# Attention in bursts of three throughout, and the first group's products in whole feature blocks of seven

## The chip, the cores and the metric

The kernel runs on one core of a Trainium2 chip. The metric is the device time of one execution in microseconds (us), the median of several runs.

## What is computed

Attention with a sigmoid in place of the softmax, then a bilinear feed-forward layer, all in float32:

```
scores = q @ kT / sqrt(64) - log(448)          # batch 8, heads 12, seq 448, head_dim 64
attn   = sigmoid(scores) @ v
x      = attn as (8*448, 12*64)                # 3584 tokens, d_model 768
out    = (((x @ w1) * (x @ w2)) @ w3) @ w_out  # d_ff 1024
```

## The kernel before

**Precision.** A float32 operand is split into a high and a low part of a reduced type (fp32r), and a product is three matmuls: high by high, high by low, low by high. One split is a cast (on ScalarE or VectorE, line 79) and a subtraction on VectorE (line 80).

**Attention** goes by items. A quad is four heads of one batch element (two pairs of heads), and there are 24 quads of seven items: three chunks of 128 keys for each pair, (0,0), (0,1), (0,2) and (1,0), (1,1), (1,2), and one short item `None`, the last 64 keys of all four heads, which stands fourth. An item has its scores (six matmuls on half the rows of the array, line 196; for the short one eight on quarter tiles, line 207) into a tile of two PSUM banks, one sigmoid of 128x896 on ScalarE (line 177) into a tile `a`, and its attend matmuls with v (four, line 220; short eight, line 228). The pool of `a` has four buffers.

**Bursts.** `sizes` cuts the 168 items into bursts. Burst k emits, in this order: the loads and splits of later pairs (`prepare`: the high cast of a pair is emitted with items (0,1) and (1,0), and its scores come three items later), the scores and sigmoids of its own items, the attends of the burst before it (`previous`), and a copy of a finished pair by ScalarE (`combine`, line 334), behind which products may follow. The order of all engines is written out by hand (`manual_schedule`): each engine works through its instructions in the order in which they are emitted.

**PSUM.** Eight banks: two `sp` tiles of two banks for scores, two `av` banks for the attends, and two upper banks. The upper pair is a tile `third` for the third item of a burst of three, or the two banks `up0` and `up1` of the products; `share_upper` closes the one pool and opens the other.

**Products** (`up`, line 533). Three of four groups of two batch elements go, as fillers, behind bursts. A group is eight feature blocks of seven products (a scheme of Strassen's kind with seven products for eight) of nine matmuls: 504 matmuls (`GROUP`). Results leave `up0`/`up1` by ScalarE copies (lines 542 and 548) and VectorE additions and multiplications (lines 500 and 503). The first group is spread over the bursts of `WINDOW`; groups 1 and 2 go whole behind the bursts of `blocks`; the last group follows the last burst.

**Weights.** w1 and w2 come as raw 64-bit words and are decoded, combined and split by the generator `weights`. One `next` is a unit: a VectorE step of the decoding (six steps for a matrix block, with the `magnitude` of the next block on ScalarE, line 89, in the fifth), a VectorE subtraction, or a `divide`: a 128x384 cast on ScalarE and a subtraction on VectorE, whose result fills one of ten slots. From the second feature block on, one block is 23 units:

```
s0 d0 t3 s1 t1 d2 s2 t2 n4 s3 d5 s4+m d1 s5 d3 | s0 d4 s1 s2 d6 s3 s4+m s5
```

Here s0 to s5 are decoding steps, m is the magnitude, t1, t2, t3 and n4 are subtractions, and d0 to d6 are the divides of the block before. 13 units lead (a start and the first block without divides) and a tail of 11 ends the 185. `take(stream, n)` takes n units. `beside` takes some behind each product. `change` holds the splits of attention results for the next group. The products of a block must find its seven divided weights, or `next(weights)` is called on the spot.

Of the kernel before, what the change touches and what calls it, by code (L numbers as in the profile page):

```python
# [25 lines left out]
def sigmoid_attention_bilinear_ffn(  # L26
# [162 lines left out]
    def scores(high, low, c, third, qk):  # L189

        at = c * P
        sp = score_banks(third)
        terms = ((high, high), (high, low), (low, high)) if high else ((qk, qk),)
        for m, (k, q) in enumerate(terms):
            for j, rows in enumerate(HEADS):
                nc.tensor.matmul(  # L196
                    sp[:, j], k[rows, 1, at:at + P], q[rows, 0],
                    start=m == 0, stop=m == len(terms) - 1,
                )
        return sp  # L200

    def short_scores(two, third):

        sp = score_banks(third)
        for u, qk in enumerate(two):
            for j, rows in enumerate(HEADS):
                nc.tensor.matmul(  # L207
                    sp[HEADS[u], j], qk[rows, 1, FULL:], qk[rows, 0], start=True, stop=True
                )
        return sp  # L210

    def attention(sp):
        a = pa.tile([P, 2, S], F32, name="a", bufs=4)
        sigmoid(a, sp)
        return a
# [18 lines left out]
    KH = NK // 2  # L234
# [111 lines left out]
    def prepare_weights():  # L346

        raw = {}

        def load(j):  # L350
            if j < 2 * NF:
                fc, i = divmod(j, 2)
                raw[j] = load_words(
                    words((w1, w2)[i], slice(fc * P, (fc + 1) * P)), p1, nc.gpsimd, 3
                )

        extras = iter(())
        for j in range(3):
            load(j)
        yield  # L360
        nxt = magnitude(raw[0], p1, 3)
        for fc in range(NF):
            fs = []
            for i in range(2):
                f = nxt
                j = 2 * fc + i
                fs.append(f)
                pops = POPS[i] if fc else (0,) * 6
                for step, _ in enumerate(decode(raw[j], f)):
                    if step == 4 and j + 1 < 2 * NF:  # L370
                        nxt = magnitude(raw[j + 1], p1, 3)
                    if step == 5:
                        del raw[j]
                        load(j + 3)
                    yield
                    for _ in range(pops[step]):
                        yield from one(extras)
            extras = finish_weights(fc, fs)
        for _ in range(sum(sum(pops) for pops in POPS)):
            yield from one(extras)  # L380
# [69 lines left out]
    def prepare_rest():  # L450

        raw = {}

        def load(i):
            if i < len(jobs):
                raw[i] = load_words(jobs[i][0], p2[0], nc.sync, 4)

        for i in range(3):
            load(i)
        for _ in range(6):  # L460
            yield
        f = magnitude(raw[0], p2[0], 3)
        for i, (_, dst) in enumerate(jobs):
            load(i + 3)
            for step, _ in enumerate(decode(raw.pop(i), f)):
                if step == 4 and i + 1 < len(jobs):
                    following = magnitude(raw[i + 1], p2[0], 3)
                yield
            nc.gpsimd.dma_start(out=dst, in_=f)
            f = following  # L470
# [3 lines left out]
    def up(g):  # L474
# [32 lines left out]
        for done, n in enumerate(stream[g * NF * 7:(g + 1) * NF * 7]):  # L507
# [55 lines left out]
            if not ending or done > 4:  # L563
                beside(g, n)
            yield

    def take(stream, n):
        done = 0
        for _ in itertools.islice(stream, n):
            done += 1  # L570
        return done
# [20 lines left out]
    assert len(quad) == TILES  # L592
    items = [(t, x) for t in range(B * NQ) for x in quad]
    GROUP = NF * 7 * KH * 3
    sizes = [3] * 18 + [2] * 28 + [3] * 5 + [2] + [3] * 5 + [2] + [3] * 8
    WINDOW = (18, 46)
    blocks = {51: 1, 57: 2}
    NBURST = len(sizes)
    starts = [sum(sizes[:k]) for k in range(NBURST + 1)]
    bursts = [items[i:i + n] for i, n in zip(starts, sizes)] + [[]]  # L600
# [3 lines left out]
    def beside(g, n):  # L604

        if g == 0:
            take(change, 1)
            take(weights, 2)
        elif not take(change, 1):
            take(rest, 2)  # L610

# [7 lines left out]
    weights = prepare_weights()  # L619
    for n in (2, 3):  # L620
        qks[n] = load_pair(n)
    filler = rest = iter(())
    change = Units(0)
# [23 lines left out]
    def attend_item(t, x, a):  # L647
        vv, vs = vvs[t]
        if x is None:
            two = (2 * t, 2 * t + 1)  # L650
            ends = [ends_of(n) for n in two]
            attend_short([accs[n] for n in two], vs, a, ends)
            for n in two:
                finish_given(n)
            return
        u, c = x
        n = 2 * t + u
        ends = ends_of(n)
        attend(accs[n], vv, u, c, a, *ends)
        finish_given(n)  # L660
        if (u, c) == (1, NC - 2):
            del vvs[t]

    def short_at(burst, at):

        shorts = [item for item in burst if item[1] is None]
        rest_of = [item for item in burst if item[1] is not None]
        if len(burst) == 3 and burst[1][1] is None:
            return shorts + rest_of if at == 0 else rest_of + shorts
        return list(burst)  # L670

    def prepare(t, x, hi_cast):

        if x == (0, 1):
            splits[2 * t + 1] = split_pair(qks[2 * t + 1], hi_cast)
        elif x == (0, 2) and t + 1 < B * NQ:
            vvs[t + 1] = load_v(t + 1)
        elif x == (1, 0) and t + 1 < B * NQ:
            splits[2 * t + 2] = split_pair(qks[2 * t + 2], hi_cast)
        elif x == (1, 1) and t + 2 < B * NQ:  # L680
            for n in (2 * t + 4, 2 * t + 5):
                qks[n] = load_pair(n)

    for k in range(NBURST + 1):
        if k == WINDOW[1]:
            phase_1.close()
            px.append(phase_x.enter_context(tc.tile_pool(name="px", bufs=1, side="left")))
            p2.append(phase_2.enter_context(tc.tile_pool(name="p2", bufs=2, side="right")))
            rest = prepare_rest()
        in_window = WINDOW[0] <= k < WINDOW[1]  # L690
        hi_cast = nc.scalar.copy if in_window or k in blocks else nc.vector.tensor_copy
        burst = bursts[k]
        for t, x in burst:
            prepare(t, x, hi_cast)
        if k < WINDOW[0]:
            if k == 1:
                next(weights)
            elif k > 1:
                take(change, 3)
                take(weights, 3 if k < 9 else 2 if k < 13 else 1)  # L700
        elif not in_window and k not in blocks and k < NBURST:
            take(change, 4 if k < 51 else 3)
        now = []
        for i, (t, x) in enumerate(short_at(burst, -1)):
            if x is None:
                sp = short_scores((qks.pop(2 * t), qks.pop(2 * t + 1)), i == 2)
            else:
                u, c = x
                if (k, i) == (0, 0):
                    high = low = None  # L710
                else:
                    high, low = splits[2 * t + u]
                sp = scores(high, low, c, i == 2, qks.get(2 * t + u))
            now.append((t, x, attention(sp)))
        if k == NBURST:
            take(change, 4)
            filler = up(NG - 1)
            take(filler, 9)
        by_place = {item[:2]: item for item in now}
        for item in previous:  # L720
            attend_item(*item)
        previous = [by_place[item] for item in short_at(burst, 0)]
        if k == WINDOW[0]:
            filler = up(0)
        if in_window:
            take(weights, 3 if k > WINDOW[0] + 1 else 0)
            done = k + 1 - WINDOW[0]
            if done % 2 == 0:
                upto, since = (GROUP * i // (WINDOW[1] - WINDOW[0]) for i in (done, done - 2))
                take(filler, upto - since)  # L730
            if k + 1 == WINDOW[1]:
                take(filler, 10)
                change = Units(1)
                take(weights, 10 ** 6)
                for n in range(RING - 1):
                    load_weights(NF * 7 + n)
        elif k in blocks:
            filler = up(blocks[k])
            take(filler, GROUP + 10)
            change = Units(blocks[k] + 1)  # L740
# [280 lines left out]
```

## Time and profile before

| | |
|---|---|
| median of three runs | 966.53 us (966.41 to 967.92) |
| the profiled execution's own time | 964.66 us |
| its span, first to last instruction | 962.9 us |
| TensorE (PE) busy | 955.6 us, 99% of the span |
| VectorE (DVE) busy | 657.1 us, 68% |
| ScalarE (ACT) busy | 400.2 us, 42% |

The median is the metric. The sum of the prediction is made against the profiled execution, whose time lies 1.76 us above its span and 1.87 us under the median. Matmul durations overlap in the trace: what one costs is read from start to start.

### The profile page before, as it was taken

The numbers are of one execution on the slowest core, as the hardware profiler recorded it, in microseconds if no ns is written. First come the engines' busy times: TensorE is split into PE (matmuls) and PEld (weight loads), VectorE is DVE, ScalarE is ACT, GpSimd is POOL, SyncE is SP. The second block draws the span as 40 slices with busy tenths as digits, with TensorE's granted clock in tenths as the row PEclk, the third lists the DMA queues.
The fourth block names the chain that finished last, engine by engine and source line by source line (L and its number), as shares of the span: only waits on it lengthen the run. The fifth ranks groups of instructions, "written<-read, shape, count | busy, mean of one in ns | idle before, by whom it ended". The sixth has DMA issues, their size and how long they took to land.

```text
span 962.9 us, 14120 instructions
## 1 busy us (share of the span) xinstructions
PE 955.6 (99%) x5236; PEld 756.4 (79%) x5236; DVE 657.1 (68%) x1060; ACT 400.2 (42%) x583; POOL 104.8 (11%) x182
## 2 busy tenths in 40 slices
PE   9999999999999999999999999999999999999998
PEld 5444666676674999957999747999999999999997
DVE  5869778887639788899888628444465657474752
ACT  7887456556548121263221474112243523232230
POOL 1110123222200012110111100211000000000000
PEclk9999999999999999999999999999999999999999
DMA  8864577776645899975999734988431033343402
GB/s 268 254 214 132 190 258 240 244 259 233 234 130 171 293 380 379 381 274 173 366 375 355 240 93 131 355 295 285 165 141 62 29 127 123 115 144 111 157 30 86
DMA packets 93781, 204.37 MB, mean 212 GB/s; under 512 B 9872, under 2 KB 57104, under 8 KB 93712
## 3 DMA queue, kind: packets, MB, share of 16 engines
q1 hardware_dynamic: 78432, 142.40, 44.0%
q0 software_dynamic: 15136, 60.83, 17.6%
q8 instruction: 42, 0.69, 0.3%
q10 hardware_dynamic: 144, 0.23, 0.1%
q14 instruction: 27, 0.22, 0.1%
HBM read 148.37 MB, written 55.05 MB: 211 GB/s over the span
## 4 chain that ended last, share of the span: by engine, by line
PE 95%; DVE 2%; DMA 1%; ACT 1%; issue 1%; SPq 0%; DVEq 0%; ACTq 0%
PE up L533 42%; PE av L220 11%; PE sp L196 8%; PE av L985 7%; PE sp L985 7%; PE up L985 7%; PE av L853 3%; PE sp L853 3%; PE av L228 2%; PE third L196 1%; PE sp L207 1%; DMA vv<-vL 1%; PE third L207 1%; ACT a L177 0%; DVE low L80 0%
## 5 line engine op out<-in xcount | busy, mean ns | idle before, releaser
L533 PE MATMUL up<-hS,w 128*128 128x448 f32 x702 | 214.6, 366 | 0.0
L533 PE MATMUL up<-hA,w 128*128 128x448 f32 x510 | 159.5, 367 | 0.3 <-ACT a L177 0.3
L177 ACT ACTIVATE a<-sp,bias 128x896 f32<-128x896 f32 x132 | 129.9, 1010 | 49.8 <-PE sp L196 24.6
L533 PEld LDWEIGHTS up<-hS,w 128*128 128x128 f32 x702 | 131.8, 188 | 14.7 <-issue 3.5
L533 PE MATMUL up<-lS,w 128*128 128x448 f32 x351 | 128.2, 365 | 0.0
L220 PE MATMUL av<-a,vv 128*64 128x448 f32 x576 | 122.8, 551 | 0.1
L533 PEld LDWEIGHTS up<-hA,w 128*128 128x128 f32 x510 | 95.8, 188 | 13.3 <-issue 4.5
L533 PE MATMUL up<-lA,w 128*128 128x448 f32 x255 | 93.2, 365 | 0.0
L220 PEld LDWEIGHTS av<-a,vv 128*64 128x64 f32 x576 | 35.5, 136 | 67.8 <-issue 67.3
L500 DVE TENSOR_TENSOR u<-up,p 128x448 f32<-128x448 f32 x64 | 39.9, 623 | 55.4 <-PE up L533 52.2
L542 ACT COPY p<-up 128x448 f32<-128x448 f32 x31 | 16.6, 534 | 146.8 <-PE up L533 141.5
L533 PEld LDWEIGHTS up<-lS,w 128*128 128x128 f32 x351 | 65.9, 188 | 5.2
L985 PE MATMUL av<-gh,wo 128*128 128x448 f32 x224 | 68.6, 367 | 0.0
L985 PE MATMUL sp<-gh,wo 128*128 128x448 f32 x224 | 68.6, 367 | 0.0
L985 PE MATMUL up<-gh,wo 128*128 128x448 f32 x224 | 68.5, 367 | 0.0
L500 DVE TENSOR_TENSOR u<-up,u 128x448 f32<-128x448 f32 x64 | 39.8, 622 | 32.4 <-PE up L533 31.8
L79 ACT CAST gh<-gf 128x896 fp32r<-128x896 f32 x40 | 35.7, 944 | 56.2 <-PE sp L985 50.0
L80 DVE TENSOR_TENSOR gl<-gf,gh 128x896 fp32r<-128x896 f32 x40 | 41.9, 1087 | 22.7 <-ACT gh L79 22.7
L80 DVE TENSOR_TENSOR low<-qk,high 128x896 fp32r<-128x896 f32 x47 | 51.3, 1091 | 7.4 <-ACT high L79 6.3
L89 ACT ACTIVATE f<-raw 128x768 f32<-128x768 f32 (+2 forms) x48 | 34.5, 718 | 50.5 <-DMA w_dram<-f 17.0
L196 PEld LDWEIGHTS sp<-high 64*128 64x128 f32 x232 | 21.9, 185 | 42.8 <-ACT a L177 31.0
L548 ACT COPY c<-up 128x448 f32<-128x448 f32 x31 | 16.6, 534 | 85.7 <-PE up L533 60.0
(145 smaller groups left out, 1778.3 us busy)
## 6 DMA issues: line engine op xcount, KB each, us to landing
w<-w_dram SPq DMA_DIRECT2D x168, 384.0 KB, 5.9
gf<-g_dram SPq DMA_DIRECT2D x16, 896.0 KB, 5.7
w_dram<-w POOLq DMA_DIRECT2D x36, 384.0 KB, 4.7
raw<-w POOLq DMA_DIRECT2D x16, 768.0 KB, 6.2
qk<-qT SPq DMA_DIRECT2D x48, 224.0 KB, 4.8
qk<-kT SPq DMA_DIRECT2D x47, 224.0 KB, 4.9
out<-o_sb SPq DMA_DIRECT2D x47, 224.0 KB, 2.0
vv<-vL SPq DMA_DIRECT2D x24, 384.0 KB, 3.5
```

The lines of the kernel that those rows point to most:

```text
L79: hi_engine(out=dst_hi, in_=src)
L80: lo_engine.tensor_tensor(out=dst_lo, in0=src, in1=dst_hi, op=ALU.subtract)
L89: nc.scalar.activation(f, raw[..., 1].bitcast(F32), AF.Abs, scale=HW_SCALE)
L177: nc.scalar.activation(dst, src, AF.Sigmoid, bias=bias[:n], scale=scale)
L196: nc.tensor.matmul(sp[:, j], k[rows, 1, at:at + P], q[rows, 0], start=m == 0, stop=m == len(terms) - 1,)
L207: nc.tensor.matmul(sp[HEADS[u], j], qk[rows, 1, FULL:], qk[rows, 0], start=True, stop=True)
L220: nc.tensor.matmul(acc[cols, :S], vv[:, c, at:at + D], a[:, j], start=start, stop=stop,)
L228: nc.tensor.matmul(acc[cols, :S], vs[HEADS[u], cols], a[HEADS[u], j], start=ends[u][0], stop=ends[u][1],)
L500: nc.vector.tensor_tensor(out=out, in0=a, in1=b, op=ALU.add)
L533: nc.tensor.matmul(a, w[:, i, kc], x, start=bool(start) and kc == 0 and m == 0, stop=bool(stop) and kc == KH - 1 and m == 2, skip_group_ch ...
L853: nc.tensor.matmul(acc, a[:, jc], w[:, jc, ms], start=(jc == 0 and m == 0), stop=(jc == NF - 1 and m == 2),)
L985: nc.tensor.matmul(acc, w[:, fc, ms], g[:, fc], start=start and fc == 0 and m == 0, stop=fc == NH - 1 and m == 2, skip_group_check=True,)
```

## The change

All bursts have three items (56 of them in place of 66). The window is 19 bursts, 18 to 36, in place of 28 bursts of two, and the first group's products are emitted as whole feature blocks, 63 matmuls each, behind bursts 19, 22, 24, 27, 29, 32, 34 and 36, in place of 36 matmuls behind every second burst. Groups 1 and 2 go behind bursts 42 and 48, of three items too, in place of bursts of two. Within the window four units of `weights` are taken behind each burst from the third on in place of three, and behind a product two, or one behind the last two products of a block.

```diff
-    sizes = [3] * 18 + [2] * 28 + [3] * 5 + [2] + [3] * 5 + [2] + [3] * 8
-    WINDOW = (18, 46)
-    blocks = {51: 1, 57: 2}
+    sizes = [3] * 56
+    WINDOW = (18, 37)
+    FIRST_BLOCKS = [WINDOW[0] + i - 1 for i in itertools.accumulate((2, 3, 2, 3, 2, 3, 2, 2))]
+    blocks = {42: 1, 48: 2}
...
         if g == 0:
             take(change, 1)
-            take(weights, 2)
+            take(weights, 2 if n % 7 < 5 else 1)
...
         elif not in_window and k not in blocks and k < NBURST:
-            take(change, 4 if k < 51 else 3)
+            take(change, 4 if k < 42 else 3)
...
         if in_window:
-            take(weights, 3 if k > WINDOW[0] + 1 else 0)
-            done = k + 1 - WINDOW[0]
-            if done % 2 == 0:
-                upto, since = (GROUP * i // (WINDOW[1] - WINDOW[0]) for i in (done, done - 2))
-                take(filler, upto - since)
+            take(weights, 4 if k > WINDOW[0] + 1 else 0)
+            if k in FIRST_BLOCKS:
+                take(filler, 7 * KH * 3)
             if k + 1 == WINDOW[1]:
                 take(filler, 10)
```

## Rows read from the trace of the kernel before

**Rows 1.** The page: the span, the busy time of three engines (time, share of the span, instructions), and the granted TensorE clock in 40 slices of the span, in tenths.

```profile
span 962.9 us, 14120 instructions
...
PE 955.6 (99%) x5236; PEld 756.4 (79%) x5236; DVE 657.1 (68%) x1060; ACT 400.2 (42%) x583; POOL 104.8 (11%) x182
...
PEclk9999999999999999999999999999999999999999
```

**Rows 2.** All waits of PE: the line that waited, the line waited for, us in total, how often, the longest.

```profile
PE up L586 <- DVE wo L579: 1.5, 1, 1.5
PE sp L196 <- DVE low L80: 0.9, 2, 0.5
PE sp L196 <- ACT a L177: 0.5, 1, 0.5
PE up L533 <- ACT a L177: 0.3, 1, 0.3
PE up L533 <- DVE c L500: 0.3, 1, 0.3
```

**Rows 3.** The window of the first group by stretches, busy time (and instructions) of each engine: from the first burst of two to the last, then the five bursts of three behind it.

```profile
88.70:286.70 198.00, 197.18 (x1118) 132.96 (x1117) 147.66 (x238) 114.55 (x169) 44.04 (x74) 1.00 0.66 221
286.70:309.00 22.30, 22.30 (x159) 10.78 (x158) 21.09 (x36) 19.34 (x28) 1.02 (x2) 1.00 0.53 170
```

**Rows 4.** PE in order of time (start, us, line, operation, count): two bursts of two, 36 products from 124.30 to 131.81, and the next bursts. The row of 135.78 holds a wait for a sigmoid.

```profile
121.23 0.47 PE L196 MATMUL sp<-high 64*128 64x448 f32 x2
...
122.65 1.72 PE L220 MATMUL av<-a,vv 128*64 128x448 f32 x8
124.30 0.47 PE L533 MATMUL up<-hS,w 128*128 128x448 f32 x1
...
131.81 0.98 PE L207 MATMUL sp<-qk 64*64 64x448 f32 x8
132.73 0.47 PE L196 MATMUL sp<-high 64*128 64x448 f32 x2
...
133.53 1.72 PE L220 MATMUL av<-a,vv 128*64 128x448 f32 x8
135.78 0.47 PE L196 MATMUL sp<-high 64*128 64x448 f32 x2 [0.53 <-ACT a L177]
136.09 0.36 PE L196 MATMUL sp<-low,high 64*128 64x448 f32 x2
...
138.39 0.97 PE L220 MATMUL av<-a,vv 128*64 128x448 f32 x4
139.29 0.47 PE L533 MATMUL up<-hA,wo 128*128 128x448 f32 x1
```

**Rows 5.** The chain of work that ended last: group 1's products (start, us, count).

```profile
313.08 102.39 PE up L533 x504
```

**Rows 6.** PE in order of time: a burst of three attended without a short item; then the last burst of three, its attends, and the first product of the last group behind it.

```profile
292.87 2.48 PE L220 MATMUL av<-a,vv 128*64 128x448 f32 x12
295.28 0.47 PE L196 MATMUL sp<-high 64*128 64x448 f32 x2
...
576.56 0.47 PE L196 MATMUL sp<-high 64*128 64x448 f32 x2
...
578.58 1.72 PE L220 MATMUL av<-a,vv 128*64 128x448 f32 x8
580.24 0.98 PE L228 MATMUL av<-a,vs 64*64 64x448 f32 x8
581.56 0.47 PE L533 MATMUL up<-hA,w 128*128 128x448 f32 x1 [0.34 <-ACT a L177]
```

**Rows 7.** ACT in order of time beside the same last burst: its three sigmoids.

```profile
578.07 1.00 ACT L177 ACTIVATE a<-sp,bias 128x896 f32<-128x896 f32 x1
579.60 1.01 ACT L177 ACTIVATE a<-sp,bias 128x896 f32<-128x896 f32 x1 [0.53 <-PE av L220]
580.51 1.00 ACT L177 ACTIVATE a<-third,bias 128x896 f32<-128x896 f32 x1
```

**Rows 8.** ACT in order of time: the copy of a pair, a magnitude and a weight cast between two bursts of three; a magnitude that waits for VectorE's subtraction; another such, a high cast and the sigmoids behind it.

```profile
50.52 0.53 ACT L334 COPY A<-av 128x448 f32<-128x448 f32 x1
50.94 0.94 ACT L89 ACTIVATE f<-raw 128x768 f32<-128x768 f32 x1
51.76 0.52 ACT L79 CAST w<-t 128x384 fp32r<-128x384 f32 x1
52.16 1.02 ACT L177 ACTIVATE a<-sp,bias 128x896 f32<-128x896 f32 x1
...
111.73 0.92 ACT L89 ACTIVATE f<-raw 128x768 f32<-128x768 f32 x1 [0.63 <-DVE wo L80]
...
133.04 0.95 ACT L89 ACTIVATE f<-raw 128x768 f32<-128x768 f32 x1 [1.30 <-DVE wo L80]
133.86 0.96 ACT L79 CAST high<-qk 128x896 fp32r<-128x896 f32 x1
134.69 1.93 ACT L177 ACTIVATE a<-sp,bias 128x896 f32<-128x896 f32 x2
```

**Rows 9.** Behind group 1's block: VectorE's last read of the product banks, and PE's first scores into `third`.

```profile
416.23 0.62 DVE L500 TENSOR_TENSOR u<-up,u 128x448 f32<-128x448 f32 x1
...
415.41 0.47 PE L196 MATMUL sp<-high 64*128 64x448 f32 x2
...
416.90 0.98 PE L207 MATMUL third<-qk 64*64 64x448 f32 x8
```

## Prediction

> **What bounds the kernel now.** The page first: TensorE (PE) is busy 955.6 of 962.9 us, the other engines far less, and the granted clock stands in its top tenth in every slice [rows 1]. So time can be won only by giving PE less to do, and is lost wherever PE waits. Its waits come second: 3.5 us in all, of which 0.5 us for a sigmoid, 0.3 us for a sigmoid ahead of products, and 0.3 us for a VectorE result [rows 2]. In the window of the first group PE has 0.82 us of idle time in 198.0 us, with VectorE busy 75% and ScalarE 58%; the five bursts of three behind it have none [rows 3]. The third view is PE in order of time, from which I take what a group of matmuls of one shape costs to enter, since that is all that cutting the same work into fewer bursts can save.
>
> **What the change saves on PE.** All matmuls stay. Scores of two items take 1.42 us (121.23 to 122.65), of one item 0.80 us (132.73 to 133.53): 0.62 us an item and 0.18 us to enter [rows 4]. Attends take 0.90 us for one item, 1.65 us for two [rows 4] and 2.41 us for three [rows 6]: 0.76 us an item, 0.14 us to enter. 36 products take 7.51 us [rows 4]; at 102.39/504 = 0.203 us each [rows 5] they are 7.31 us, so 0.20 us to enter. Bursts go from 66 to 56 and product blocks from 16 to 10: 10 x (0.18 + 0.14) + 6 x 0.20 = 4.4 us. The short items' own groups stay 24 and 24. Two waits of the window go with its bursts of two: the scores at 135.78 come 0.60 us after 133.53 + 1.65 [rows 4], and 0.3 us for VectorE [rows 2]. Saved: 5.3 us.
>
> The Trainium skill, "TensorEngine Tiling (Array Packing)", Tiling Modes (Key Properties), says that a change of tiling mode drains the array, and "TensorE: Matmul & The Clock Gate", Single matmul latency, puts the fixed part of one matmul at 166 ns. By these an estimate for the 26 groups saved is 4.3 us, where the rows give 4.4.
>
> **What it adds: products behind a burst of three.** Before, the window's bursts of two never touch the upper two banks, and both whole-group blocks stand behind bursts of two. After, each of the ten blocks follows a burst whose third scores lie in the two banks that its first product writes. So that product waits for the sigmoid that reads `third`. The trace shows this once, at the end: the first product of the last group starts at 581.56, after a wait for the sigmoid that ran from 580.51 to 581.51 [rows 6, 7].
>
> Why that sigmoid is late there, with nothing else on ScalarE: six tiles `a` would be alive (three to be attended, three being made), and there are four. The second sigmoid starts only at 579.60, 1.02 us after the attends began at 578.58, released by them, and the third 0.91 us later [rows 7]. So the third starts 1.93 us after the attends' start, and the product 2.98 us after it. The attends themselves last 2.41 us without a short item [rows 6], and with one 1.66 + 0.92 = 2.58 us, taking the short one at its score's 0.92 us [rows 4]. Least wait per block: 0.57 us without, 0.40 us with a short item. Block bursts 27, 32, 34 and 48 attend a short item, the other six don't: 4 x 0.40 + 6 x 0.57 = 5.0 us. With bursts of two there were four tiles for four, and nothing to wait for.
>
> **What else stands ahead of that sigmoid.** In the window the high cast of a pair is on ScalarE, and weight casts and magnitudes are emitted behind each burst, so ahead of the next burst's sigmoids. Before, the 36 products (7.5 us) gave ScalarE time to catch up; after, bursts of 4.4 to 4.7 us follow each other twice or three times. Start to start a pair's copy takes 0.42 us, a magnitude 0.82, a weight cast 0.40, a high cast 0.83 [rows 8], a sigmoid 0.91 [rows 7].
>
> Count from the start of a burst: scores end at 2.02 us (578.58 - 576.56 [rows 6]), or 2.32 with a short item scored; the third sigmoid is due 1.93 later, so the first may start as late as 2.14 (2.44) without harm. A burst on time leaves ScalarE at 4.86 (5.16), behind that come the copy, the burst's weight work and the next high cast, and PE goes on at scores + attends.
>
> The weight work follows from counting units: 35 are taken before the window, each block takes 12, each burst from 20 on four. That puts, per burst, a magnitude and two casts (1.62 us) at 20, 25, 28 and 31; a magnitude and one (1.22) at 33; three casts (1.20) at 35; two (0.80) at 23 and 26; one (0.40) at 21 and 30; none at 18. Worked through:
> - block 19: 4.86 + 0.42 + 0.83 - 4.60 = 1.51, below 2.44: on time.
> - 22: burst 21's first sigmoid at 4.86 + 0.42 + 1.62 + 0.83 - 4.60 = 3.13, its end 2.72 later at 5.85; 22's at 5.85 + 0.42 + 0.40 + 0.83 - 4.43 = 3.07: 0.63 late.
> - 24: 2.31, on time.
> - 27: burst 26 at 3.13, then 5.85 + 0.42 + 0.80 + 0.83 - 4.73 = 3.17 against 2.14: 1.03 late.
> - 29: 4.86 + 0.42 + 1.62 + 0.83 - 4.43 = 3.30: 0.86 late.
> - 32, without a high cast: 5.16 + 0.42 + 1.62 - 4.73 = 2.47: 0.33 late.
> - 34: 5.16 + 0.42 + 1.22 + 0.83 - 4.73 = 2.90: 0.76 late.
> - 36: 2.88: 0.44 late.
> - 42 and 48 have no weight work and fall under block 19's sum.
>
> Together 4.05 us. The bound below is nothing (ScalarE not late), the bound above adds a magnitude's wait for VectorE's subtraction just ahead of it, 0.63 us in one row, 1.30 in another, none in a third [rows 8]; three of the chains (bursts 25, 28, 33) hold that pair, so up to 3 x 0.63 = 1.9 us more. I take half, 0.95.
>
> ScalarE's casts stand in the way only because it keeps its order. The Trainium skill says so ("PSUM — Partial Sum Buffer", Engine vs sequencer instructions: ScalarE's queue is strict FIFO). By that rule the late part counts; an engine that took the sigmoid first would leave 5.0 - 5.3 = -0.3 us.
>
> **What I cost at nothing.** VectorE inside a block: its mean instruction is 147.66/238 = 0.62 us [rows 3], so an addition and two units behind each product are 1.86 us against 9 x 0.203 = 1.83 us of products, and the last two products take one unit less. It stays level; if each block's last addition came 0.62 us later, the next third scores would wait, since behind group 1's block the addition ends at 416.85 and those scores start at 416.90 [rows 9]: up to 8 x 0.62 = 5.0 us. Units: each block finds its weights, since before blocks 0 to 7 some 35, 59, 79, 103, 123, 147, 167 and 187 can have been taken, and the divides fall due at 33 + 23 per block, the last few of which `beside` supplies three or more products ahead. Loads per burst are those of the bursts of three behind the window, in which PE never idles [rows 3]. `change` is taken as often between the same events. The stores and the five weight loads at the window's end stand behind the last block on POOL and SP as before, with five bursts until group 1 needs them.
>
> **The sum.** Waits 5.0 + 4.05 + 0.95 = 10.0 us, saved 5.3: +4.7 us. The profiled execution of 964.66 us becomes 969.4; the median, 1.87 above it, 966.53 + 4.7 = 971.2 us.
>
> **The rivals.**
> - *Only the tile wait is paid* (ScalarE catches up in time): -0.3 us, 966.2. For it: ScalarE is busy only 58% of the window [rows 3]. Against: a magnitude and a high cast ahead of the sigmoids already made PE wait at 135.78 [rows 4, 8], with more room than there will be. With half the lateness: +1.7 us. 22%, no measurable change.
> - *The change wins its entries* (the other side): the waits stay under 3.4 us, since the sigmoid behind the block's burst is not late. Place: the first product of each block; it decides at 0.34 us per block, under the smallest wait of rows 6 and 7. With no wait at all, -5.3 us: 961.2. For it: 2 of the 10 blocks stood behind bursts without any wait before, though of two. Against: the row of 581.56. The Trainium skill ("Perfetto Trace Analysis", Matmuls) wants independent groups in different banks, so that one's evacuation overlaps the next; here the third item and the products share theirs, and the rule speaks for the wait. 12%.
> - *VectorE becomes late too*: blocks pay another 0.6 us at the third scores behind them, +9.7 us, 976.2. For it: no margin in rows 9. Against: one unit less behind the last two products. 10%.
> - My forecast, +2.5 to +7 us: 56%.
>
> **How the numbers follow.** About 0.2%, 1.9 us, is what can be told from no change: 964.6 to 968.5 counts as the same. Slower: 56 + 10 = 66%. Same: 22%. Faster: 12%. The range reaches from the lower edge of the tile-wait case, 964.8, to 975.5, short of the VectorE case; some 12% are left below it and 8% above. My own case alone spans 969.0 to 973.5.
>
> **What would show it.** Right: PE waits of products (line 533) for the sigmoid (line 177), ten of them besides the one at the end, near 10 us in all, from 0.4 to 0.6 us at blocks 19, 24, 42 and 48 to 1.4 or more at 27 and 29, where ScalarE shows magnitude, casts and high cast just ahead of the sigmoids. Scores groups 56, PE's busy time down some 4 us. The prediction is wrong if the first product of a block follows the attends at once, if these waits sum to 5 us (ScalarE not late), or if new waits stand elsewhere: third scores behind VectorE, or products behind weights.

## The result: 0.74% slower

The changed kernel takes 973.0 us (median of six, 970.05 to 975.37) against 965.96 us for the kernel before in the same comparison: ratio 1.0074, 95% interval 1.0059 to 1.0089, which is 5.7 to 8.6 us. The forecast was slower, +4.7 us and 971.2 us. The direction and the place are right, the size falls short, and the part that is missing was not among the rivals. Two executions among those of the experiments ran at a mean granted clock of 0.61 and 0.66 and took over 1330 us; no ratio below contains them.

The profiled execution took 970.05 us, 5.4 more than that of the kernel before. The page of the changed kernel, its span and the busy time:

```profile
span 968.3 us, 14147 instructions
...
PE 950.0 (98%) x5236; PEld 758.4 (78%) x5236; DVE 656.4 (68%) x1058; ACT 400.7 (41%) x585; POOL 104.4 (11%) x182
```

PE is busy 5.6 us less than in [rows 1], and idle 18.3 us where it was 7.3. Where the idle time came from is in the view of all waits of PE, laid out as [rows 2]:

```profile
PE up L533 <- ACT a L177: 10.7, 11, 2.2
PE up L586 <- DVE wo L579: 1.5, 1, 1.5
PE sp L196 <- DVE low L80: 0.9, 2, 0.5
PE third L196 <- DVE low L80: 0.6, 1, 0.6
PE third L196 <- ACT a L177: 0.6, 1, 0.6
PE up L533 <- DVE u L500: 0.3, 1, 0.3
PE sp L196 <- ACT a L177: 0.2, 1, 0.2
```

Eleven waits of products for a sigmoid, 10.7 us: ten blocks, and the one of 0.34 us at the end that was there before. PE in order of time, the first product of each block, with the idle time ahead of it in brackets, and one other pair of waits (89.73 and 90.76), to which I come back:

```profile
89.73 0.47 PE L196 MATMUL third<-high 64*128 64x448 f32 x2 [0.56 <-ACT a L177]
90.76 0.47 PE L196 MATMUL third<-low,high 64*128 64x448 f32 x2 [0.57 <-DVE low L80]
99.30 0.47 PE L533 MATMUL up<-hA,w 128*128 128x448 f32 x1 [0.56 <-ACT a L177]
127.22 0.47 PE L533 MATMUL up<-hA,wo 128*128 128x448 f32 x1 [1.11 <-ACT a L177]
150.18 0.47 PE L533 MATMUL up<-hA,w 128*128 128x448 f32 x1 [0.56 <-ACT a L177]
...
179.42 0.47 PE L533 MATMUL up<-hA,w 128*128 128x448 f32 x1 [1.35 <-ACT a L177]
...
204.39 0.47 PE L533 MATMUL up<-hA,wo 128*128 128x448 f32 x1 [2.23 <-ACT a L177]
...
232.09 0.47 PE L533 MATMUL up<-hA,w 128*128 128x448 f32 x1 [0.71 <-ACT a L177]
...
256.38 0.47 PE L533 MATMUL up<-hA,w 128*128 128x448 f32 x1 [1.88 <-ACT a L177]
...
279.63 0.47 PE L533 MATMUL up<-hA,wo 128*128 128x448 f32 x1 [0.96 <-ACT a L177]
...
320.95 0.47 PE L533 MATMUL up<-hA,w 128*128 128x448 f32 x1 [0.56 <-ACT a L177]
...
451.77 0.47 PE L533 MATMUL up<-hA,w 128*128 128x448 f32 x1 [0.40 <-ACT a L177]
```

The forecast for these ten, block by block, was 0.57, 1.20, 0.57, 1.43, 1.43, 0.73, 1.16, 1.01, 0.57 and 0.40 us. Eight of ten agree within 0.1 us. The two that don't are blocks 29 and 34, by 0.80 and 0.72 us. ACT in order of time ahead of block 29 says why:

```profile
196.88 1.00 ACT L177 ACTIVATE a<-third,bias 128x896 f32<-128x896 f32 x1
197.76 0.53 ACT L334 COPY A<-av 128x448 f32<-128x448 f32 x1
198.18 0.53 ACT L79 CAST w<-f 128x384 fp32r<-128x384 f32 x1
199.45 0.95 ACT L89 ACTIVATE f<-raw 128x768 f32<-128x768 f32 x1 [0.74 <-DVE w L80]
200.31 0.49 ACT L79 CAST w<-t 128x384 fp32r<-128x384 f32 x1
200.71 0.93 ACT L79 CAST high<-qk 128x896 fp32r<-128x896 f32 x1
201.55 1.88 ACT L177 ACTIVATE a<-sp,bias 128x896 f32<-128x896 f32 x2
203.34 0.99 ACT L177 ACTIVATE a<-third,bias 128x896 f32<-128x896 f32 x1
```

One burst's third sigmoid, a pair's copy, the weight cast, a magnitude that waits 0.74 us for VectorE's subtraction, a second cast, the high cast, and only then the three sigmoids of the block's burst, the last of which ends at 204.33. The product starts at 204.39.

### The profile page after: what moved, and what is told of

The parts are those of the page before. It is cut to its first block, busy times and chain, and to the rows that moved or that the text cites. A ratio compares the mean times of both kernels' runs of the same rounds, so it can differ in the third digit from the quotient of the medians.

```text
span 968.3 us, 14147 instructions
## 1 busy us (share of the span) xinstructions
PE 950.0 (98%) x5236; PEld 758.4 (78%) x5236; DVE 656.4 (68%) x1058; ACT 400.7 (41%) x585; POOL 104.4 (11%) x182
## 4 chain that ended last, share of the span: by engine, by line
PE 89%; ACT 5%; DVE 3%; issue 2%; DMA 1%; DVEq 0%; ACTq 0%
PE up L533 42%; PE av L220 7%; PE av L984 7%; PE sp L984 7%; PE up L984 7%; PE sp L196 6%; ACT a L177 4%; PE av L852 3%; PE sp L852 3%; PE third L196 2%; PE av L228 2%; PE third L207 1%; DMA w_dram<-w 1%; ACT high L79 1%; DVE low L80 1%
## 5 line engine op out<-in xcount | busy, mean ns | idle before, releaser
L177 ACT ACTIVATE a<-sp,bias 128x896 f32<-128x896 f32 x112 | 111.8, 1012 | 78.0 <-PE sp L196 39.7
L220 PE MATMUL av<-a,vv 128*64 128x448 f32 x576 | 120.6, 549 | 0.0
L177 ACT ACTIVATE a<-third,bias 128x896 f32<-128x896 f32 x56 | 56.4, 1007 | 0.0
L533 PEld LDWEIGHTS up<-lA,w 128*128 128x128 f32 x255 | 47.9, 188 | 3.6
```

Source lines behind the costliest of these rows:

```text
L177: nc.scalar.activation(dst, src, AF.Sigmoid, bias=bias[:n], scale=scale)
L220: nc.tensor.matmul(acc[cols, :S], vv[:, c, at:at + D], a[:, j], start=start, stop=stop,)
L533: nc.tensor.matmul(a, w[:, i, kc], x, start=bool(start) and kc == 0 and m == 0, stop=bool(stop) and kc == KH - 1 and m == 2, skip_group_ch ...
```

## The experiments

My theory: products wait for the sigmoid that reads the shared banks, held back partly by the four tiles `a` and partly by ScalarE's other work ahead of it. The rivals: whole blocks cost time by themselves (VectorE, weights), or the entries saved are worth less than read from the rows.

**High casts on VectorE.**

```diff
-        hi_cast = nc.scalar.copy if in_window or k in blocks else nc.vector.tensor_copy
+        hi_cast = nc.scalar.copy if k in blocks else nc.vector.tensor_copy
```

> The changed kernel with the high casts of the window's pairs on VectorE in place of ScalarE, blocks 42 and 48 as they are. Theory (two parts: four tiles of sigmoid results hold the third sigmoid back by 0.4 to 0.57 us per block, ScalarE's other work the rest): the late part falls by 0.83 us per burst, the waits of products from 10.7 to between 5.5 and 7 us, each of them 0.4 to 1.0 us; 4 to 5 us faster than the changed kernel, if VectorE's added 0.62 us per pair makes no new wait. Rival (ScalarE's order has nothing to do with it, only the tiles count): no change against the changed kernel.

Ratio to the kernel before 1.0037 (1.0022 to 1.0053): some 3.6 us faster than the changed kernel, a little under what was expected. PE's waits, and two first products in order of time, blocks 27 and 29:

```profile
PE up L533 <- ACT a L177: 7.1, 11, 1.4
```

```profile
178.39 0.47 PE L533 MATMUL up<-hA,w 128*128 128x448 f32 x1 [0.40 <-ACT a L177]
...
202.56 0.47 PE L533 MATMUL up<-hA,wo 128*128 128x448 f32 x1 [1.40 <-ACT a L177]
```

Block 27 falls from 1.35 us to its least wait of 0.40, block 29 by 0.83 us, one cast's worth; 7.1 us are left, just above the range expected. So the high casts alone carry 3.6 us of the 10.7; of what is left, 5.0 us are the least waits of the forecast, 0.3 us the end, and the other 1.8 us stand where weight casts and magnitudes are ahead. VectorE's added work made one new wait, 0.56 us of scores for a low part at 173.51.

**Five tiles of sigmoid results**, with one raw buffer less to make room.

```diff
-        a = pa.tile([P, 2, S], F32, name="a", bufs=4)
+        a = pa.tile([P, 2, S], F32, name="a", bufs=5)
...
-                    words((w1, w2)[i], slice(fc * P, (fc + 1) * P)), p1, nc.gpsimd, 3
+                    words((w1, w2)[i], slice(fc * P, (fc + 1) * P)), p1, nc.gpsimd, 2
...
-        for j in range(3):
+        for j in range(2):
             load(j)
...
-                        load(j + 3)
+                        load(j + 2)
```

> The changed kernel with five tiles for sigmoid results in place of four; the room comes from raw weights, two buffers in place of three. Theory: the third sigmoid can start 0.91 us earlier wherever ScalarE is free, so the waits at blocks 19, 24, 32, 42, 48 and at the end vanish, and those at 22, 27, 29, 34 and 36 stay at 0.3 to 1.7 us: 3.5 to 5 us in place of 10.7, 6 us faster than the changed kernel, within 2 us of the kernel before. Rival (the tiles do not hold the sigmoid back): waits as in the changed kernel.

Ratio 1.0033 (1.0019 to 1.0046): some 4 us faster than the changed kernel, where 6 had been expected, and 3.2 us above the kernel before. Six waits for the sigmoid are left of eleven, 6.3 us: those at blocks 19, 24, 32, 48 and at the end are gone, as the theory has it. But more is left than expected, 0.38 us at block 42 among it: with the tiles out of the way ScalarE's own queue is the limit at blocks 22 to 36 (0.68 to 1.92 us). The missing raw buffer cost something too: a wait of scores of 1.49 us near the start, behind a magnitude that waited for its raw words.

This trace holds something that the forecast had left out. PE waited 1.92 us ahead of block 29 (its first product starts at 204.75). The stretches around that: their length, the busy time of the engines, then the granted clock, DMA share and GB/s at the end:

```profile
203.00:204.70 1.70, 0.00 (x0) 0.00 (x0) 0.64 (x1) 1.70 (x3) 0.00 (x0) 1.00 1.03 344
204.70:205.90 1.20, 1.15 (x5) 1.08 (x6) 0.77 (x2) 0.81 (x2) 0.70 (x1) 0.94 0.93 355
205.90:209.10 3.20, 3.20 (x10) 2.81 (x10) 2.78 (x5) 0.94 (x2) 0.70 (x2) 0.50 0.81 269
209.10:212.00 2.90, 2.90 (x16) 2.68 (x15) 1.88 (x4) 0.90 (x1) 0.68 (x2) 0.99 0.57 215
```

About 1.1 us after the products start again the granted clock falls to 0.50, the lower of the two levels (1.2 GHz), stays there for 3.2 us, and comes back: 1.7 us of work lost behind a pause of 1.92 us.

**Five tiles and high casts on VectorE** (both edits).

> Both: five tiles, and the window's high casts on VectorE. Theory: nothing is left of the waits for the sigmoid but some 1 us at block 29; 10 us faster than the changed kernel, 4 to 5 us faster than the kernel before, which is what the fewer group entries give. Rival (the entries saved are not worth 4.4 us, or whole blocks bring other costs): no faster than the kernel before though the waits are gone.

Ratio 0.9996 (0.9984 to 1.0008): 7.5 us faster than the changed kernel, and no faster than the kernel before. The waits for the sigmoid fell to 1.5 us. What took the place of the expected 4 us is in the trace: the same start-up wait, 1.86 us here, with a lower clock behind it (0.50 for 3.2 us), and a wait of products of 1.05 us for a copy by ScalarE. So in this trace the experiment spoiled its own gain, and I looked for another way to the same end.

**The shared banks for the second item.** In bursts that products follow, the second item gets the two upper banks, so the sigmoid that products wait for is no longer the last.

```diff
+        third_at = 1 if k in FIRST_BLOCKS or k in blocks else 2
...
-                sp = short_scores((qks.pop(2 * t), qks.pop(2 * t + 1)), i == 2)
+                sp = short_scores((qks.pop(2 * t), qks.pop(2 * t + 1)), i == third_at)
...
-                sp = scores(high, low, c, i == 2, qks.get(2 * t + u))
+                sp = scores(high, low, c, i == third_at, qks.get(2 * t + u))
```

> The changed kernel, but in a burst that products follow the second item, not the third, gets the two banks that it shares with the products, so its sigmoid is the second of three on ScalarE and ends 0.91 us sooner. Theory: every wait of products for the sigmoid falls by 0.91 us or to nothing: from 10.7 us to some 3 us, left at blocks 22 (0.2), 27 (0.4), 29 (1.3) and 34 (1.0) and at the end (0.3); 7 us faster than the changed kernel, 1 to 3 us faster than the kernel before. Rival (the wait is for ScalarE's whole burst, not for the tile in the shared banks): waits as in the changed kernel.

Ratio 1.0019 (1.0009 to 1.0029): 5.3 us faster than the changed kernel, still 1.8 us slower than the one before. The waits for the sigmoid fell as expected, from 10.7 to 2.6 us (1.34 of them at block 29). Others came: 1.2 us of products for VectorE (0.3 in the changed kernel) and 1.5 us of the shared banks' scores for the sigmoid of the burst before, which now come one item sooner. This trace also has 1.4 us of attends for a DMA near the start, far ahead of the edit.

**The same with high casts on VectorE.**

> The same, and the window's high casts on VectorE. Theory: of the waits for the sigmoid under 1 us is left, at block 29 and the end; 9 to 10 us faster than the changed kernel, 3 to 4 us faster than the kernel before. Rival (the entries saved are worth less than 4.4 us): within 1 us of the kernel before, though the waits are gone.

Ratio 0.9987 (0.9978 to 0.9996), 964.96 us: faster than the changed kernel by 8.4 us and than the kernel before by 0.4 to 2.1 us. PE's waits:

```profile
PE sp L196 <- DVE low L80: 1.5, 3, 0.6
PE up L533 <- DVE u L500: 1.0, 2, 0.8
PE up L533 <- ACT a L177: 0.8, 2, 0.5
```

The products' waits for the sigmoid are gone as the theory has it, under 1 us; the rival's number (within 1 us of the kernel before) is nearer to the time. Part of the shortfall is not a wait. The chain of work that ended last has the whole-group products as one piece each (start, us, count). In the changed kernel:

```profile
320.95 102.41 PE up L533 x504
```

and in this one, group 1 and the last group (93.03 us in the chain of the kernel before and of the changed one):

```profile
312.82 104.34 PE up L533 x504
445.17 102.42 PE up L533 x504
592.35 94.99 PE up L533 x459
```

The same 504 matmuls on the same data ran at 0.207 us each, not 0.203, with no wait and a granted clock of 1.00; 3.9 us in the two pieces. All three kernels with the banks given to the second item show it in the same two pieces, the kernel with five tiles too, and the kernel before didn't in its trace. The long pause below shows it in group 1 alone, with the buffers and the order of products of the changed kernel, so it comes without the banks' change too. Each kernel has one trace at the upper clock, so it may go by execution as well as by kernel; the cause is open.

**Bursts of two ahead of products**, blocks whole.

```diff
-    sizes = [3] * 56
+    sizes = [3] * 18
+    for n in (2, 3, 2, 3, 2, 3, 2, 2):
+        sizes += [3] * (n - 1) + [2]
+    sizes += ([3] * 5 + [2]) * 2 + [2] * 2 + [3] * 9
```

> The changed kernel with whole feature blocks and the same units of weights, but each burst that products follow has two items, so no third scores share the product banks: 60 bursts in place of 56. Theory (products wait for the sigmoid of the third item): the waits of products for that sigmoid go from 10.4 us at ten blocks to under 0.5 us, four more bursts cost 4 x 0.32 = 1.3 us, so some 9 us faster than the changed kernel and 3 to 5 us faster than the kernel before. Rival (whole blocks overload VectorE or come ahead of their weights): the blocks are as whole as before, so the time stays within 2 us of the changed kernel, 5 us or more above the kernel before.

Ratio 0.9998 (0.9989 to 1.0007): 7 us faster than the changed kernel, which settles that the third item ahead of the products, not whole blocks, made it slow; but not faster than the kernel before. The same kernel again, for its trace:

> The kernel with two items in the bursts that products follow, again, for a profile at the upper clock level. Its first run was 0.5 us under the kernel before where 3 to 5 us had been expected. Theory (entries are worth 0.14 to 0.20 us each): no waits of products for the sigmoid, PE busy some 4 us under the kernel before, and a named new wait or a late stretch that takes back 3 us. Rival (the entries are worth less): PE busy as in the kernel before and no new wait.

Ratio 1.0010 (0.9999 to 1.0021). The sigmoid's waits are down to the 0.3 us at the end, and PE's busy time to 953.2 us: 2.4 us under the kernel before, where the forecast's prices make 3.1 for six bursts and six blocks fewer (the 4 us expected left out the four added bursts). The new wait has a name: PE's products wait 2.8 us for VectorE, at blocks 24, 27 and 32. VectorE in order of time at block 27:

```profile
175.71 0.96 DVE L113 SCALAR_TENSOR_TENSOR raw<-raw 128x768 f32<-128x768 uint32 x1
176.70 0.96 DVE L117 TENSOR_TENSOR f<-f,raw 128x768 f32<-128x768 f32 x1
177.58 0.62 DVE L500 TENSOR_TENSOR u<-up,p 128x448 f32<-128x448 f32 x1
```

and PE there:

```profile
176.48 0.37 PE L533 MATMUL up<-hA,w 128*128 128x448 f32 x1
178.25 0.47 PE L533 MATMUL up<-hS,w 128*128 128x448 f32 x1 [1.40 <-DVE u L500]
```

Two decoding steps taken behind the first product stand ahead of the second product's addition on VectorE, and the fourth product needs that bank.

**The same units, later in the block.**

```diff
-            take(weights, 2 if n % 7 < 5 else 1)
+            take(weights, (0, 2, 2, 2, 2, 1, 3)[n % 7])
```

On the bursts of two:

> The kernel with bursts of two ahead of products, with the same twelve units of weights per block, but none behind its first product, two behind each of the next four, one behind the sixth and three behind the last. In the trace of the kernel with bursts of two, the result of a block's second product waits on VectorE behind weight units, and the fourth product then waits for it (1.40, 1.00 and 0.40 us). Theory (what the saved entries and sigmoid waits gave went into these waits): they fall from 2.8 us to under 1 us, and the time by some 2 us, to 1 to 3 us under the kernel before. Rival (they come from the whole blocks' own pace, whatever the order): 2 us or more of them stay.

The waits of products for VectorE went from 2.8 us to none, so it was their order. The time did not move: ratio 0.9999 (0.9990 to 1.0008). 1.2 us came back as scores that wait for a sigmoid ahead of block 24. This trace has no slower products, and its account closes: PE is busy 2.3 us less than in the kernel before and idle 2.6 us more. On the second-item kernel:

> The kernel with the shared banks for the second item and high casts on VectorE, with the units of a block placed in the same way. Theory: its two waits for VectorE (0.77 and 0.23 us) go, the rest stays; 1 to 3 us under the kernel before. Rival (units moved to the end of a block delay the low parts of the next burst): new waits of scores for VectorE of over 1 us, no faster than the kernel before.

The waits for VectorE in blocks went too; ratio 0.9985 (0.9976 to 0.9995), 964.71 us, as fast as without this edit, and again a little faster than both kernels.

**A longer pause.** The third sigmoid is made three times over in the eight block bursts of the window.

```diff
             now.append((t, x, attention(sp)))
+            if i == 2 and k in FIRST_BLOCKS:
+                for _ in range(2):
+                    sigmoid(now[-1][2], sp)
```

> The changed kernel with the sigmoid of the third item made three times over in the eight bursts of the window that products follow: 2 x 0.91 us more of ScalarE ahead of each of these blocks, and no other work. Theory (PE waits for that sigmoid and nothing else): eight waits longer by 1.82 us each, 14.6 us on the time, if PE's clock stays at its upper level. With the second price seen in the five-tile kernel (a pause of 1.92 us, then some 3.4 us at half the clock, 1.7 us lost), pauses of 2.4 to 4.1 us cost up to 1.7 us more each: 15 to 28 us in all, and the granted clock of the span falls under 0.995. Rival (the sigmoid is hidden elsewhere): under 5 us.

Ratio 1.0348: 27 us above the changed kernel. PE's waits and busy time:

```profile
PE up L533 <- ACT a L177: 27.6, 11, 4.3
```

```profile
PE 963.8 (96%) x5236; PEld 767.8 (77%) x5236; DVE 656.7 (66%) x1058; ACT 416.8 (42%) x601; POOL 104.9 (11%) x182
```

The waits grew by 16.9 us, 2.1 at each of the eight blocks (I had reckoned 1.82: a repeated sigmoid costs 1.04 us). PE's busy time grew by 13.8 us on the same matmuls. Three of the eight blocks, laid out as the stretches above:

```profile
130.00:147.00 17.00, 13.83 (x57) 12.21 (x54) 10.64 (x18) 6.81 (x11) 3.04 (x5) 0.80 0.69 249
158.00:175.00 17.00, 14.08 (x71) 12.12 (x69) 12.77 (x22) 7.51 (x12) 3.06 (x5) 1.00 0.80 260
189.00:206.00 17.00, 13.57 (x65) 11.99 (x58) 12.41 (x21) 8.18 (x12) 4.38 (x7) 0.90 0.65 213
```

Six of the eight pauses, of 2.65 to 4.32 us, come with a stretch at half the clock that loses 1.6 to 3.4 us; two, of 2.92 and 3.04 us, do not. The mean granted clock of the span is 0.986, and 0.014 x 998.8 = 14.0 us, a part of it inside the pauses. Not all of the 13.8 us is the clock's: group 1 stands behind these blocks, and its products are the slower ones here, 2.0 us of it at a granted clock of 1.00.

```profile
349.56 104.42 PE up L533 x504
```

So the 16.9 us of longer waits brought some 12 us more at the lower clock.

## Why the prediction was right, and where it fell short

- **What is saved on PE** (5.3 us): right, a little under. PE's busy time fell by 5.6 us where 4.4 were forecast for entries, and the wait for the sigmoid within the window fell from 0.5 to 0.2 us. The 0.3 us for VectorE stayed.
- **Products behind a burst of three** (5.0 us): right. The blocks without a late ScalarE wait 0.56 and 0.40 us, and a fifth tile removes them at 19, 24 and 48; at 42, where a high cast is left on ScalarE, 0.38 us stay.
- **What else stands ahead of that sigmoid** (4.05 us): right in size and place; taking one cast away takes 0.83 us off block 29.
- **The magnitude's wait** (0.95 us, half its bound): mis-sized. Half was a guess between nothing and 1.9. It comes whole at blocks 29 and 34 and not at all at 27, 1.5 us, though a magnitude ahead of burst 26 waits 0.62 us too. With it the ten waits make 10.3 us, where the sum had 10.0.
- **VectorE at nothing**: held in the changed kernel, 0.3 us. With the sigmoid's wait gone (bursts of two) 2.8 us of waits for VectorE appear; that the wait had given VectorE the time is argued. It is the rival that I had placed behind blocks and that stands inside them.
- **`change` and the splits at nothing**: wrong by 1.1 us. Burst 18 used to have two items; its third now opens the next quad, whose low part VectorE finishes only at 90.71 (the wait at 90.76). At 89.73 the trace names a sigmoid, which ended at 89.67; VectorE's cast of the high part ended at 89.58, so without that sigmoid the scores would have come hardly sooner.
- **The clock**: the step that failed. I noted that it stood at its top level throughout and priced pauses by their length alone. The profiled execution of the changed kernel kept its clock (mean 1.000), and its +5.4 us is near the forecast of +4.7: the 1.1 us of the new quad and the 0.3 us more of waits are in part made good by the 0.6 us more saved. The five others have mean clocks of 0.996 to 0.998 and take 971.6 to 975.4 us: 0.002 x 970 = 1.9 us lost, one stretch at half the clock, or twice that. Pauses of 1.88 and 2.23 us stand at blocks 34 and 29, and one of 1.92 us was seen ahead of such a stretch in the kernel with five tiles. The other runs point the same way: a mean clock of 0.998 or less comes in 4 of 10 executions with five tiles (longest pause in the trace 1.92 us), in 3 of 12 with both edits (1.86 us), in 1 of 71 executions of the six kernels whose longest pause is 1.5 us or less, and never in the kernel before. That a given execution's 1.9 us follows one of these two pauses is argued, since the one with a trace kept its clock. So the median lies 7.0 us up, not 4.7.

Still open: with the waits for the sigmoid removed, the best kernels gain 1.3 to 1.4 us on the kernel before, not 4. In the trace of the first of them (shared banks for the second item, high casts on VectorE) 2.7 us are more idle time of PE, 3.9 us the slower products, whose cause no run here shows.

## What to carry to other kernels

When work is regrouped into larger pieces, list the buffers that each boundary used to keep apart: here a third item in shared banks put a sigmoid, and everything ahead of it on ScalarE, on PE's path at ten places. Saved entries are worth 0.14 to 0.20 us each and are lost to one wait of half a microsecond; count both before regrouping. A wait removed lets the next engine in line show its own lateness, so removing it by moving one tile is worth trying first, and the views of waits are to be read again after each step.

## What the runs showed that was not expected

- A pause of PE of 1.9 us can be followed by 3.2 us at half the granted clock (1.7 us lost); of eight pauses of 2.65 to 4.32 us six came with such a stretch, and one of 2.23 us did not.
- The same products run at 0.203 us or at 0.207 us each for a hundred microseconds on end at a granted clock of 1.00: 102.4 or 104.4 us for 504 of them. Group 1 ran at the slower pace in five of eleven traces, group 2 in none.
- Of sigmoids into the same tile one after the other (the long pause), the second and third cost 1.04 us each where sigmoids into different tiles follow each other by 0.91 us [rows 7].
